# Packed attention and two mixtures on one core: first values in rows of nine tokens, a fold's copies in two turns, later keys by two queues

## The chip, the cores and the metric

The kernel runs on one core of a Trainium2 chip. The metric is the device time of one execution in microseconds (us). TensorE is called PE here (its weight loads PEld), VectorE DVE, ScalarE ACT, GpSimd POOL, SyncE SP.

## The reference

Four batches of eight heads attend to 576 tokens of 64 numbers through 32 packed queries p; the result, 2304 tokens by 512, goes through two layers of two matrices each. Cut to what matters:

```python
p_packed = sm_attn(p, k, v)                 # softmax(p k^T / 8) v: 32 rows a head
out = sm_attn(q, p_packed, p_packed)        # 576 rows a head
x = out.transpose(0, 2, 1, 3).reshape(2304, 512)
h = x @ moe_w_in;   g = h * tanh(log1p(exp(h)));   x = g @ moe_w_out     # d_ff 2048
h = x @ moe2_w_in;  g = where(h > 0, h, exp(h) - 1);  return g @ moe2_w_out
```

## The kernel before

Large matmuls are done in fp32r on a high and a low half of each operand: `split_hi` (L259) writes the high half, `split_lo` (L265, L267) the rest, and three products (high by high, high by low, low by high) stand for one.

**Attention of a batch.** `load_heads` (L348) brings k, q and v of two heads on 128 partitions. For batch 0, k and q come as rows (head, 64 groups of tokens) of nine tokens, 2304 contiguous bytes (L362); v comes by two DMAs a pair of heads (L355), five of the nine tokens to the first 64 partitions and four to the others (`RUNS`). `scores1` makes the scores of the packed queries and their exp (L463), one tile e1 for each half s of the heads; `transpose_a1` turns it on PE (L490) and copies it out, on DVE at L394 (ACT's copies are L392); `packed` multiplies by v (L515), scales, turns the result on PE and copies it to the tile PT, s by s. `scores2` multiplies the queries, transposed on DVE (L404), by PT (L569), turns the scores on DVE (`turn_s`, L598), and makes softmax and its split.

**First mixture.** The packed values are folded into the first matrix: `fold` (L651) multiplies PT by a quarter of w_in (matmul L662) and copies the two halves of the product out in two splits each (high: ACT, L259; low: DVE, L267). `gemm1` (L696 to L698), `mish` (t by ACT L706, gh by ACT L392, gl by DVE L714) and `gemm2` (L732 to L734) run in steps over 16 slices of d_ff and 8 blocks of 288 tokens. Meanwhile the second layer's first matrix is decoded into sums (w2c) and written to memory by POOL (`combine`, L321), and `reload_w1i` (L335) brings the first matrix again for the next batch's folds; y, the result of the first layer, is written by POOL too (L753).

**Second mixture.** `quartet` makes products over w2c (`product`, L828), elu, and splits; `gemm4` (L914) multiplies by the last matrix and, at the end, copies to ob (ACT L392, DVE L394 by turns) and writes out (L935). `second` decodes the last matrix in chunks of four raw tiles.

**What sets the order.** `startup` goes by the list `ORDER`, written by hand (r is a raw tile's load, L157; d a step of a decode, of which L194 is on ACT and L216 and L232 on DVE; 0T, 0V the turn and copy of e1, 0K the value products, 0P, 0U, 0W their scaling, turn and copy, 0S and 0t the second scores and their turn, f00 the first fold). Behind it `mixture1` and `mixture2` post closures in turn (a `Track` runs one post of a fold or of an attention step at a time), and a scheduler then places each instruction. A queue's instructions run in order; `pm` hands out the PSUM tiles.

## Time and profile before

| what | us |
|---|---|
| median of three runs | 779.54 |
| lowest and highest | 777.58, 779.99 |
| the profiled execution | 780.52 |
| its span in the trace | 778.7 |
| PE busy, DVE, ACT, POOL | 747.2, 529.1, 396.6, 104.3 |

The profile is of one execution. An engine is busy while an instruction of its own runs; a wait row names the instruction that waited and the one that released it; the chain of waits follows the last instruction back to its causes. The granted clock is a share of full speed: 1.00 is the 2.4 GHz level and 0.50 the 1.2 GHz level.

### The profile page before, as it was taken

To read this page: it belongs to the slowest core of one execution; us is meant where nothing else is said; L and a number is where in the kernel's file an instruction comes from. 1 tells how busy PE (TensorE), PEld (TensorE's weight loads), DVE (VectorE), ACT (ScalarE), POOL (GpSimd) and SP (SyncE) were. 2 spreads that over 40 slices of the span, in tenths; PEclk is the share of its full clock that TensorE was granted. 3 is DMA by queue.
4 is the path that set the end of the run, shared out by engine and by line. 5 is a ranking of instruction groups with operands and counts; after the bars stand their busy time and mean duration, and the time that the engine had idled before them with its cause. 6 is when DMAs were issued, how large, how long until landed. Compare 5 with 4: busy or idle time off the path is not lost.

```text
span 778.7 us, 13963 instructions
## 1 busy us (share of the span) xinstructions
PE 747.2 (96%) x5173; PEld 668.4 (86%) x5173; DVE 529.1 (68%) x1135; ACT 396.6 (51%) x840; POOL 104.3 (13%) x199
## 2 busy tenths in 40 slices
PE   7299999999999999999999999999999999999997
PEld 4198888898888988999998899888998889899985
DVE  5899977744953669886667878876455676545553
ACT  2799916473656457765644445534232354323332
POOL 1100000120120124752000003133000001000000
PEclk9699999999999999999999999999999999999999
DMA  8998746695483465877656325456343347333312
GB/s 283 412 358 262 186 101 193 181 253 159 112 253 77 126 202 182 281 234 247 233 199 202 116 109 196 155 189 204 109 115 122 102 139 240 108 110 116 128 54 82
DMA packets 95107, 138.81 MB, mean 178 GB/s; under 512 B 57920, under 2 KB 63616, under 8 KB 95040
## 3 DMA queue, kind: packets, MB, share of 16 engines
q1 hardware_dynamic: 83104, 105.73, 44.0%
q0 software_dynamic: 10208, 29.90, 10.5%
q10 hardware_dynamic: 1728, 2.29, 0.9%
q8 instruction: 41, 0.67, 0.4%
q14 instruction: 26, 0.21, 0.1%
HBM read 109.58 MB, written 28.31 MB: 177 GB/s over the span
## 4 chain that ended last, share of the span: by engine, by line
PE 79%; ACT 6%; DVE 6%; DMA 5%; issue 2%; SPq 1%; ACTq 0%; POOL 0%; DVEq 0%
PE o L914 24%; PE h L828 21%; PE acc L733 7%; PE acc L732 7%; PE acc L734 6%; PE h L696 3%; PE h L698 3%; PE h L697 3%; PE pm L662 2%; DMA w_dr<-w2c 2%; SPq L379 1%; DMA raw_w1i<-in_moe_w_in_dram 1%; ACT t L706 1%; ACT gh L259 1%; DMA k<-in_k_dram 1%
## 5 line engine op out<-in xcount | busy, mean ns | idle before, releaser
L828 PE MATMUL h<-y,w2c 128*128 128x384 f32 x1008 | 196.0, 337 | 1.8 <-ACT hs L392 1.2
L828 PEld LDWEIGHTS h<-y,w2c 128*128 128x128 f32 x1008 | 178.9, 188 | 12.3 <-ACT hs L392 2.0
L733 PE MATMUL acc<-gl,w1oh 128*128 128x288 f32 x512 | 151.1, 296 | 0.4 <-DVE gl L714 0.3
L734 PE MATMUL acc<-gh,w1ol 128*128 128x288 f32 x512 | 150.1, 295 | 0.0
L732 PE MATMUL acc<-gh,w1oh 128*128 128x288 f32 x512 | 148.7, 297 | 0.0
L914 PE MATMUL o<-w2ol,gh 128*128 128x512 f32 x288 | 113.0, 392 | 0.0
L914 PE MATMUL o<-w2oh,gh 128*128 128x512 f32 x288 | 109.1, 394 | 0.1
L914 PE MATMUL o<-w2oh,gl 128*128 128x512 f32 x288 | 108.1, 392 | 0.5 <-DVE gl L265 0.4
L733 PEld LDWEIGHTS acc<-gl,w1oh 128*128 128x128 f32 x512 | 96.1, 188 | 5.1 <-issue 2.3
L732 PEld LDWEIGHTS acc<-gh,w1oh 128*128 128x128 f32 x512 | 95.0, 188 | 6.0 <-issue 4.5
L734 PEld LDWEIGHTS acc<-gh,w1ol 128*128 128x128 f32 x512 | 96.0, 188 | 0.8 <-issue 0.8
L714 DVE TENSOR_TENSOR gl<-t,gh 128x288 fp32r<-128x288 f32 x128 | 57.2, 451 | 42.7 <-ACT gh L392 41.7
L696 PE MATMUL h<-a2h,gh 128*128 128x288 f32 x256 | 77.8, 304 | 3.5 <-ACT t L706 2.1
L706 ACT ACTIVATE t<-h 128x288 f32<-128x288 f32 x128 | 51.1, 405 | 56.0 <-PE h L698 53.2
L321 POOL DMA_DIRECT2D w_dr<-w2c x112 | 59.8, 540 | 138.0 <-DVE w2c L267 129.7
L698 PE MATMUL h<-a2h,gl 128*128 128x288 f32 x256 | 76.6, 300 | 0.0
L697 PE MATMUL h<-a2l,gh 128*128 128x288 f32 x256 | 76.4, 299 | 0.0
L259 ACT ACTIVATE gh<-t 128x384 fp32r<-128x384 f32 x96 | 49.6, 522 | 44.3 <-DVE t L839 42.5
L265 DVE TENSOR_TENSOR gl<-t,gh 128x384 fp32r<-128x384 f32 x96 | 52.8, 554 | 15.5 <-ACT gh L259 14.2
L914 PEld LDWEIGHTS o<-w2oh,gl 128*128 128x128 f32 x288 | 53.9, 188 | 10.9 <-DVE gl L265 1.2
L914 PEld LDWEIGHTS o<-w2ol,gh 128*128 128x128 f32 x288 | 54.1, 188 | 10.3
L392 ACT ACTIVATE gh<-t 128x288 fp32r<-128x288 f32 x112 | 49.4, 443 | 24.7 <-PE acc L734 22.8
(134 smaller groups left out, 1072.6 us busy)
## 6 DMA issues: line engine op xcount, KB each, us to landing
w2c<-w_dr SPq DMA_DIRECT2D x84, 512.0 KB, 3.6
w_dr<-w2c POOLq DMA_DIRECT2D x112, 128.0 KB, 3.3
w1r<-w_dr SPq DMA_DIRECT2D x24, 512.0 KB, 5.9
raw_w1i<-in_moe_w_in_dram SPq DMA_DIRECT2D x16, 512.0 KB, 10.5
raw_w1o<-in_moe_w_out_dram SPq DMA_DIRECT2D x16, 512.0 KB, 9.7
raw_w2i<-in_moe_w_in_dram SPq DMA_DIRECT2D x16, 512.0 KB, 4.3
raw_w2o<-in_moe_w_out_dram SPq DMA_DIRECT2D x16, 512.0 KB, 3.7
y_dr<-y POOLq DMA_DIRECT2D x16, 288.0 KB, 3.8
```

The lines of the kernel that those rows point to most:

```text
L259: nc.scalar.activation(out=hi, in_=val, func=ACTF.Copy, scale=factor)
L321: nc.gpsimd.dma_start(out=w2_dr[n // 2][:, n % 2, p], in_=d[x][:, i].bitcast(F32))
L696: nc.tensor.matmul(out=hp, lhsT=wh, rhs=xh, start=(kt == 0), stop=False)
L697: nc.tensor.matmul(out=hp, lhsT=wh, rhs=xl, start=False, stop=False)
L698: nc.tensor.matmul(out=hp, lhsT=wl, rhs=xh, start=False, stop=(kt == 1))
L706: nc.scalar.activation(out=d["t"], in_=d["h"], func=ACTF.Mish)
L714: nc.vector.tensor_tensor(out=gl, in0=d["t"], in1=gh.bitcast(F32), op=ALU.subtract)
L732: nc.tensor.matmul(out=o, lhsT=wh[:, cs], rhs=gh, start=first, stop=False)
L733: nc.tensor.matmul(out=o, lhsT=wh[:, cs], rhs=gl, start=False, stop=False)
L734: nc.tensor.matmul(out=o, lhsT=wl[:, cs], rhs=gh, start=False, stop=last)
L828: nc.tensor.matmul(out=hp, lhsT=w[:, p, a, :], rhs=y[:, b, :], start=start and p == 0 and i == 0, stop=p == 1 and i == 2, skip_group_check ...
L914: nc.tensor.matmul(out=o, lhsT=x[:, ts], rhs=y, start=(n == 1 and i == 0), stop=(n == NK and i == 2))
```

## The change

- Batch 0's v is loaded as k is, one DMA for a pair of heads, in rows of nine tokens. The exp tiles of batch 0 hold five and four groups of tokens for both halves s. A new function `values0` turns them (nine transposes for ten), multiplies by v in nine pieces of 64 rows for each head half (72 matmuls for 80) and copies PT once for twice.
- `whole`: a fold's copies are posted in two turns, high and low of one half, then of the other, in place of one.
- k of batches 2 and 3: of the DMAs of 32 x 9 x 32 (L379), those of the second 32 columns (x = 1) go by POOL.
- `product` and `gemm4` use one order for all blocks j: high by high, high by low, low by high. Before, block 2 of `gemm4` began with the low half of g.
- The last of the six final copies is done half by ACT, half by DVE.
- `second` asks for the raw tiles of the next chunk earlier.

```diff
 ORDER = """
-0k0 lq00 0k1 lq01 lq02 0k2 0k3 lq03 tp0 0A0 r0 0A1 0M0 r1 0E0 0M1 r2 0E1 0T0 0R0 0V0@ 0T1 0R1 r3 0K0 r4 0V1 r5
+0k0 lq00 0k1 lq01 lq02 0k2 0k3 lq03 tp0 0A0 r0 0A1 0M0 r1 0E0 0M1 r2 0E1 0T0 0R0 0T1 0V0@ 0R1 r3 r4 0V1 0K0 r5
...
-    def pm():
-        turn[0] += 1
-        if starting[0] and turn[0] % 3:
+    def pm(kind=None):
+        turn[0] += not kind
+        if kind == "a" or not kind and starting[0] and turn[0] % 3:
             t = ps_a.tile([128, 2, 512], F32, tag="acc", name="pm")
...
-        if nm == "v":
+        if nm == "v" and b:
             t = home([128, 2, 5, D], F32, f"{nm}{b}_{g}")
...
-                        eng.dma_start(
+                        (nc.gpsimd if x else eng).dma_start(
...
-            e1 = E1[b, s] = small([128, 5 * 128], F32, f"e1_{b}_{s}")
+            if not s or b:
+                E1[b, s] = small([128, 5 * 128], F32, f"e1_{b}_{s}")
+            if not s and not b:
+                E1[b, 1] = small([128, 5 * 128], F32, f"e1_{b}_1")
+            e1 = E1[b, s]
...
+                if not b:
+                    e1, r = E1[b, x], 64 * s
...
+    def values0():
+
+        d = {}
+        NC = NB // 2
+
+        def turn(x):
+            pm("a")
+            ps = d["t", x] = last_pair[0].rearrange("p h n -> p (h n)")
+            e1 = E1.pop((0, x))
+            for i in range(RUNS[x][2]):
+                cols = slice(128 * i, 128 * i + 128)
+                nc.tensor.transpose(out=ps[:, cols], in_=e1[:, cols], identity=ident)
+
+        def out(x, eng):
+            n = RUNS[x][2]
+            a1 = d["a", x] = small([128, n, 128], F32, f"a1t0_{x}")
+            evac(eng, a1, d["t", x][:, 0:n * 128].rearrange("p (c x) -> p c x", x=128))
+
+        def pe():
+            ps = d["k"] = pm("p")
+            for i in range(NC):
+                a1 = d["a", i // 5][:, i % 5, :]
+                for g in (3, 2, 1, 0):
+                    for s in range(2):
+                        r = slice(64 * s, 64 * s + 64)
+                        nc.tensor.matmul(
+                            out=ps[s][32 * g:32 * g + 32, 0:D], lhsT=a1[r, 32 * g:32 * g + 32],
+                            rhs=vt_in[0, g][r, 2 * i:2 * i + 2, :], start=(i == 0), stop=(i == NC - 1),
+                        )
+            for g in range(4):
+                vt_in.pop((0, g))
+
+        def scaled(s, eng="v"):
+            m = d["m", s] = st.tile([128, D], F32, tag="pv", name="pv")
+            rs = RS.pop((0, s))[:, 1:2]
+            if eng == "v":
+                nc.vector.tensor_scalar(out=m, in0=d["k"][s][:, 0:D], scalar1=rs, scalar2=None, op0=ALU.mult)
+            else:
+                nc.scalar.activation(out=m, in_=d["k"][s][:, 0:D], func=ACTF.Copy, scale=rs)
+
+        def turn2(s):
+            y = d["k"][0]
+            turns = [(slice(0, 64), 64 * s, 256)]
+            turns += [(slice(32 * x, 32 * x + 32), 64 * s + 32 * (1 - x), 384) for x in range(2)]
+            for cols, r, c in turns:
+                w = cols.stop - cols.start
+                nc.tensor.matmul(out=y[r:r + w, c:c + 128], lhsT=d["m", s][:, cols], rhs=ident)
+
+        def final(eng="v"):
+            PT[0] = ptp.tile([128, 256], F32, tag="pt", name="pt")
+            evac(eng, PT[0], d["k"][0][:, 256:512])
+
+        return turn, out, pe, scaled, turn2, final
...
-            d[0], d[1] = pm(), pm()
+            d[0], d[1] = pm("a"), pm("a")
...
-            for i, (a, b) in enumerate(((0, 0), (0, 1), (1, 0)) if j != 1 else ((0, 0), (1, 0), (0, 1))):
+            for i, (a, b) in enumerate(((0, 0), (0, 1), (1, 0))):
...
-            trio = [(gh, wh), (gh, wl), (gl, wh)]
-            if j == 1:
-                trio = [(gh, wh), (gl, wh), (gh, wl)]
-            if j == 2:
-                trio = [(gl, wh), (gh, wh), (gh, wl)]
-            for i, (x, y) in enumerate(trio):
-                nc.tensor.matmul(out=o, lhsT=x[:, ts], rhs=y, start=(n == 1 and i == 0), stop=(n == NK and i == 2))
+            nc.tensor.matmul(out=o, lhsT=gh[:, ts], rhs=wh, start=(n == 1), stop=False)
+            nc.tensor.matmul(out=o, lhsT=gh[:, ts], rhs=wl, start=False, stop=False)
+            nc.tensor.matmul(out=o, lhsT=gl[:, ts], rhs=wh, start=False, stop=(n == NK))
...
-                evac("av"[t % 2], ob, o)
+                if j == 2 and half and t == 2:
+                    evac("a", ob[:, 0:256], o[:, 0:256])
+                    evac("v", ob[:, 256:512], o[:, 256:512])
+                else:
+                    evac("av"[t % 2], ob, o)
...
-        for kt in range(2):
-            load_vt(0, kt)
+        for g in range(4):
+            load_heads(v, vt_in, 0, g, "v", (nc.sync, nc.scalar)[g % 2])
...
-                groups = (
-                    ("AMER", scores1(b, s)), ("TV", transpose_a1(b, s, "v")), ("KPUW", packed(b, s)),
-                )
+                groups = [("AMER", scores1(b, s))]
+                if b:
+                    groups += [("TV", transpose_a1(b, s, "v")), ("KPUW", packed(b, s))]
                 for names, fs in groups:
                     for n, f in zip(names, fs):
                         step(f"{b}{n}{s}", f, "a" if n in "VPW" else None)
+            if not b:
+                turned, copied, pe, scaled, turned2, final = values0()
+                for s in range(2):
+                    step(f"0T{s}", lambda s=s: turned(s))
+                    step(f"0V{s}", lambda eng="v", s=s: copied(s, eng), "a")
+                    step(f"0P{s}", lambda eng="v", s=s: scaled(s, eng), "a")
+                    step(f"0U{s}", lambda s=s: turned2(s))
+                step("0K0", pe)
+                step("0W0", final, "a")
...
-        for r in rows[:2]:
+        for r in rows[:2 if c < 2 else 0]:
...
-            if x < 2:
-                todo.append(lambda r=rows[x + 2]: load_raw("w2o", r, 0))
+            n = rows[x + 2] if x < 2 else 4 * (c + 1) + 2 * (x - 2)
+            if x < 2 or 0 < c < 3:
+                todo.append(lambda n=n: load_raw("w2o", n, 0))
...
-            return [f[0], lambda: [f[i]() for i in (1, 3, 2, 4)]]
+            return [f[0]] + [lambda x=x: (f[1 + x](), f[3 + x]()) for x in range(2)]
...
```

SP at the start, before (v and raw tiles are the values and the weights as they come; pr is p; ACT issues the other half in the same way):

```order
L362 DMA k_0_171<-in_k_dram 128x576
L362 DMA k_2_175<-in_k_dram 128x576
L993 DMA pr_149<-in_p_dram 32x4x64 x2
L355 DMA v_0_184<-in_v_dram 64x2x320
L355 DMA v_1_187<-in_v_dram 64x2x320
L355 DMA v_2_190<-in_v_dram 64x2x320
L355 DMA v_3_193<-in_v_dram 64x2x320
L362 DMA q_1_202<-in_q_dram 128x576
L362 DMA q_3_210<-in_q_dram 128x576
L157 DMA raw_w1i_0_230<-in_moe_w_in_dram 128x1024
```

and now:

```order
L362 DMA k_0_171<-in_k_dram 128x576
L362 DMA k_2_175<-in_k_dram 128x576
L1053 DMA pr_149<-in_p_dram 32x4x64 x2
L362 DMA v_0_184<-in_v_dram 128x576
L362 DMA v_2_188<-in_v_dram 128x576
L362 DMA q_1_198<-in_q_dram 128x576
L362 DMA q_3_206<-in_q_dram 128x576
L157 DMA raw_w1i_0_226<-in_moe_w_in_dram 128x1024
```

The four value issues of SP are two, in the form of the keys, and queries and raw tiles follow two issues earlier.

POOL at batch 3's keys, where one set of w2c ends and the next begins, before (y_dr is the first layer's result):

```order
L321 DMA w_dr_117<-w2c 128x256
L753 DMA y_dr_105<-y_0_2569 128x576
L753 DMA y_dr_105<-y_1_2573 128x576
L321 DMA w_dr_111<-w2c 128x256
L321 DMA w_dr_114<-w2c 128x256
```

and now:

```order
L321 DMA w_dr_117<-w2c 128x256
L813 DMA y_dr_105<-y_0_2582 128x576
L813 DMA y_dr_105<-y_1_2586 128x576
L379 DMA k_0_3049<-in_k_dram 32x9x32 x4
L379 DMA k_1_3058<-in_k_dram 32x9x32 x4
L379 DMA k_2_3129<-in_k_dram 32x9x32 x4
L379 DMA k_3_3138<-in_k_dram 32x9x32 x4
L321 DMA w_dr_111<-w2c 128x256
L321 DMA w_dr_114<-w2c 128x256
```

The half of the keys stands between y and the first w2c of the next set.

ACT at the last fold of batch 3, before (gh_3 is the fold's high half, t and gh the mish step):

```order
L259 ACTIVATE w2c<-dec 128x2x128
L259 ACTIVATE gh_3_3000<-pm 128x512 x2
L706 ACTIVATE t_3158<-h_3151 128x288
L392 ACTIVATE y_0_3176<-acc_2605 128x288
L392 ACTIVATE gh_3160<-t_3158 128x288
L392 ACTIVATE y_1_3180<-acc_2606 128x288
L706 ACTIVATE t_3196<-h_3189 128x288
```

and now:

```order
L259 ACTIVATE w2c<-dec 128x2x128
L259 ACTIVATE gh_3_3067<-pm 128x512
L392 ACTIVATE y_0_3199<-acc_2613 128x288
L392 ACTIVATE y_1_3203<-acc_2614 128x288
L259 ACTIVATE gh_3_3067<-pm 128x512
L766 ACTIVATE t_3219<-h_3212 128x288
L259 ACTIVATE w2c<-sums 128x2x128
```

The halves of gh_3 have both copies of y between them; t follows them as before.

## Rows read from the trace of the kernel before

**Rows 1.** The page: busy by engine; a PE group: busy, mean ns | idle before, releaser.

```profile
PE 747.2 (96%) x5173; PEld 668.4 (86%) x5173; DVE 529.1 (68%) x1135; ACT 396.6 (51%) x840; POOL 104.3 (13%) x199
...
L914 PE MATMUL o<-w2oh,gl 128*128 128x512 f32 x288 | 108.1, 392 | 0.5 <-DVE gl L265 0.4
```

**Rows 2.** The chain of waits, 0 to 60 us: start, length, what.

```profile
11.41 8.90 DMA raw_w1i<-in_moe_w_in_dram
```

**Rows 3.** Windows: PE, PEld, DVE, ACT, POOL busy, granted clock, DMA share, GB/s.

```profile
5.00:11.00 6.00, 4.61 (x71) 2.71 (x69) 4.57 (x9) 0.73 (x3) 0.00 (x0) 1.00 0.91 243
36.70:42.00 5.30, 5.21 (x28) 3.15 (x28) 5.15 (x11) 5.27 (x11) 0.82 (x2) 0.50 1.02 411
```

**Rows 4.** Issues of first values and keys: ns min/median/max, first to last start.

```profile
L355 SPq DMA_DIRECT2D v<-in_v_dram x9: 595/603/713, 4.7 to 61.4; - x9
...
L362 SPq DMA_DIRECT2D k<-in_k_dram x6: 328/328/416, 0.7 to 36.9; - x6
```

**Rows 5.** Timeline of PE, 11 to 34 us: start, length, work, [idle before <-releaser].

```profile
11.39 2.40 PE L490 MATMUL pm<-ident,e 128*128 128x128 f32 x10 [1.53 <-ACT e L463]
13.72 2.16 PE L515 MATMUL pm<-v,a1t 128*32 128x64 f32 x80
...
17.73 1.89 PE L569 MATMUL pm<-qT,pt 32*32 32x288 f32 x46 [0.58 <-DVE pt L394]
20.39 0.72 PE L569 MATMUL pm<-qT,pt 32*32 32x288 f32 x18 [0.76 <-issue]
33.57 1.11 PE L662 MATMUL pm<-w1v,pt 64*32 64x512 f32 x8 [12.45 <-DVE w1v L232]
```

**Rows 6.** Timeline of DVE, 13 to 23 us.

```profile
14.63 2.74 DVE L404 STREAM_TRANSPOSE qT<-q 128x576 f32<-128x576 f32 x4
17.30 0.84 DVE L394 COPY pt<-pm 64x256 f32<-64x256 f32 x2
...
21.03 0.43 DVE L216 TENSOR_SCALAR w1v<-raw_w1i 128x512 int32<-128x512 int32 x1 [1.65 <-ACT raw_w1i L194]
...
22.21 1.21 DVE L598 STREAM_TRANSPOSE x<-pm 128x288 f32<-128x288 f32 x3
```

**Rows 7.** Timelines of PE and ACT at 224 to 228 us.

```profile
227.24 0.40 PE L696 MATMUL h<-a2h,gh 128*128 128x288 f32 x1 [1.54 <-ACT t L706]
...
226.29 0.60 ACT L259 ACTIVATE gh<-pm 128x512 fp32r<-128x512 f32 x1 [0.76 <-DVE gl L267]
226.78 0.41 ACT L706 ACTIVATE t<-h 128x288 f32<-128x288 f32 x1
```

**Rows 8.** Chain at 150 to 170, PE at 166, waits of 210 to 230.

```profile
157.32 6.20 DMA w_dr<-w2c
...
167.24 0.76 PE L490 MATMUL pm<-ident,e 128*128 128x128 f32 x5 [0.84 <-ACT e L463]
...
ACT w2c L259 <- DMA w_dr<-w2c: 7.7, 3, 5.0
```

**Rows 9.** Later keys: issues, the window that holds most of batch 2's, SP's timeline.

```profile
L379 SPq DMA_DIRECT2D k<-in_k_dram x64: 312/453/1966, 110.2 to 221.1; - x64
...
125.30:140.10 14.80, 14.80 (x130) 13.02 (x128) 9.88 (x19) 6.71 (x16) 1.08 (x2) 1.00 0.69 171
...
208.79 0.35 SPq L157 DMA_DIRECT2D raw_w2i<-in_moe_w_in_dram  x1
209.18 12.42 SPq L379 DMA_DIRECT2D k<-in_k_dram  x20
```

**Rows 10.** POOL's w2c writes: issues, and the first of the second set.

```profile
L321 POOL DMA_DIRECT2D w_dr<-w2c x112: 539/539/559, 149.1 to 354.3; - x112
...
197.68 1.07 POOL L321 DMA_DIRECT2D w_dr<-w2c  x2 [11.49 <-DVE w2c L267]
```

**Rows 11.** The end: timelines of PE and ACT.

```profile
769.51 0.50 PE L914 MATMUL o<-w2oh,gl 128*128 128x512 f32 x1 [0.43 <-DVE gl L265]
...
773.00 1.57 ACT L392 ACTIVATE ob<-o 128x512 f32<-128x512 f32 x3 [1.89 <-DVE ob L394]
```

More of the change, by code (lines that the diff above doesn't have):

```diff
@@ L42 @@
 ORDER = """
-0k0 lq00 0k1 lq01 lq02 0k2 0k3 lq03 tp0 0A0 r0 0A1 0M0 r1 0E0 0M1 r2 0E1 0T0 0R0 0V0@ 0T1 0R1 r3 0K0 r4 0V1 r5
-0q0 0K1 0P0@ r6 0q1 0U0 0P1@ 0q2 r7 0q3 0U1 0W0 r8 d0.0 0W1 0S0 d0.1 r9 d0.3 d0.4 d1.0 d1.1 d1.3 d1.4 0t0 r10
-d2.0 0t1 d2.2 r11 0X2 d3.0 0X1 0Y2 r12 0N2 d4.0 d4.2 r13 0X0 0Y1 d5.0 0B2 0Y0 d2.1 d2.4 0H2 0N0 r14 d6.0 0L2
-0B0 r15 0X3 0H0 d7.0 0L0 0Y3 r16 d3.1 d7.2 d4.1 d8.0 d3.3 d3.4 r17 d4.4 d7.1 f00 d9.0 d8.1 d4.5 d9.2 d8.3 d8.4
-fh001 fh000 lk12 d9.1 d9.4 d10.0 fl000 d10.2 lk10 fl001 d11.0 d10.1 d10.4 g0 d11.2 lk13 d6.1 d12.0 d5.1 g1
@@ L48 @@
-d11.1 d11.4 m0 lk11 d6.3 f01 d5.3 m1 pr1 0N1 g2 h0 h1 fh011 g3 l0 m2 fl011 fh010 G0 h2 l1 d5.4 fl010 d13.0 r18
-d5.5 g4 lw100 l2 r19 0B1 m3 G1 m4 0N3 d6.4 d12.2 d6.5 r20 g5 d13.2 h3@ d12.1 G2 h4 m5 l3 d7.4 l4 r21 d12.4
-d7.5 g6 d15.0 r22 d12.5 G3 r23 d13.1 m6 0B3 0H1 d13.4 h5@ 0L1 g7 0H3 d13.5 d14.0 G4 0L3 h6@ 1k3 d14.2 l5 g8 m7
-r24 l6 d15.2 d14.1 G5 h7 d15.1 m8 r25 d14.4 l7 d15.4 g9 d14.5 h8 d15.5 d16.0 G6 1k0 m9 l8 d19.0 tp1 g10 G7 1k1
-m10 r26 h9 1k2 d19.2 l9 g11 d16.2 h10@ y7.0 d20.0 1A0 l10 r27 y7.1 y7.2 m11 g12 y7.3 d18.0 1M0 G8 d19.1 d19.4
@@ L53 @@
-m12 1E0 d18.1 g13 d20.1 G9 h11@ d18.3 d18.4 d17.0 l11 1R0 1A1 d16.1 d16.4 d17.2 d20.3 h12 G10 d17.1 d17.4 lv11
+0k0 lq00 0k1 lq01 lq02 0k2 0k3 lq03 tp0 0A0 r0 0A1 0M0 r1 0E0 0M1 r2 0E1 0T0 0R0 0T1 0V0@ 0R1 r3 r4 0V1 0K0 r5
+0q0 0P0@ r6 0q1 0U0 0P1@ 0q2 r7 0q3 0U1 0W0 r8 d0.0 0S0 d0.1 r9 d0.3 d0.4 d1.0 d1.1 d1.3 d1.4 0t0 r10 d2.0 0t1
+d2.2 r11 0X2 d3.0 0X1 0Y2 r12 0N2 d4.0 d4.2 r13 0X0 0Y1 d5.0 0B2 0Y0 d2.1 d2.4 0H2 0N0 r14 d6.0 0L2 0B0 r15
+0X3 0H0 d7.0 0L0 0Y3 r16 d3.1 d7.2 d4.1 d8.0 d3.3 d3.4 r17 d4.4 d7.1 f00 d9.0 d8.1 d4.5 d9.2 d8.3 d8.4 fh001
@@ new lines @@
+fh000 lk12 d9.1 d9.4 d10.0 fl000 d10.2 lk10 fl001 d11.0 d10.1 d10.4 g0 d11.2 lk13 d6.1 d12.0 d5.1 g1 d11.1
+d11.4 m0 lk11 d6.3 f01 d5.3 m1 pr1 0N1 g2 h0 h1 fh011 g3 l0 m2 fl011 fh010 G0 h2 l1 d5.4 fl010 d13.0 r18 d5.5
+g4 lw100 l2 r19 0B1 m3 G1 m4 0N3 d6.4 d12.2 d6.5 r20 g5 d13.2 h3@ d12.1 G2 h4 m5 l3 d7.4 l4 r21 d12.4 d7.5 g6
+d15.0 r22 d12.5 G3 r23 d13.1 m6 0B3 0H1 d13.4 h5@ 0L1 g7 0H3 d13.5 d14.0 G4 0L3 h6@ 1k3 d14.2 l5 g8 m7 r24 l6
+d15.2 d14.1 G5 h7 d15.1 m8 r25 d14.4 l7 d15.4 g9 d14.5 h8 d15.5 d16.0 G6 1k0 m9 l8 d19.0 tp1 g10 G7 1k1 m10
@@ L54 @@
+r26 h9 1k2 d19.2 l9 g11 d16.2 h10@ y7.0 d20.0 1A0 l10 r27 y7.1 y7.2 m11 g12 y7.3 d18.0 1M0 G8 d19.1 d19.4 m12
+1E0 d18.1 g13 d20.1 G9 h11@ d18.3 d18.4 d17.0 l11 1R0 1A1 d16.1 d16.4 d17.2 d20.3 h12 G10 d17.1 d17.4 lv11
 d25.0 l12 d26.0 1M1 d20.4 lv12 g14 d23.0 d25.1 d20.5 G11 1E1 lv10 d26.1 d25.3 d25.4 d24.0 lv13 1R1 f02 m13
```

## The prediction

> **What bounds the kernel now.** I read the page first: PE is busy 747.2 of 778.7 us [rows 1], so outside the start, the end and a few holes the time is PE's own work, and nearly all of that the change leaves alone (8 of the first batch's 80 value matmuls and one transpose go). Copies, DMAs and waits off PE therefore earn only where PE stands still; each part is judged by the PE hole that it touches. Four places have one.
>
> *The start, 0 to 36.7 us.* The chain of waits shows transfers first: the longest piece is a raw weight tile that is 8.90 us in flight [rows 2]. In the windows [rows 3] only 243 GB/s move from 5 to 11 us, when the values come in, and 411 later. The value DMAs take 0.60 us each to issue, the keys 0.33 [rows 4]. On PE [rows 5] transposes run from 11.39, value products from 13.72, the second scores from 17.73 to 21.11; then PE is idle 12.45 us until the first fold at 33.57. On DVE [rows 6] the query transposes (14.63, 2.74 us) end at 17.37, the copy of PT follows, a decode that begins at 21.03 has waited 1.65 us for a raw tile, and the turn of the scores starts at 22.21, behind that decode. From there DVE has hardly a gap up to the fold.
>
> *The clock.* From 36.7 to 42 us the granted clock is 0.50, the 1.2 GHz level, behind the long idle [rows 3]; later, as in 125.3 to 140.1, it is 1.00 [rows 9].
>
> *The middle.* PE stands 1.54 us at 227.24, because ACT did the two halves of a fold's copy one behind the other, 0.76 us of that waiting for DVE, with the mish step's t behind them [rows 7]. And 0.84 us at 167.24, where ACT had been held by a transfer of w2c [rows 8].
>
> *The end.* PE waits 0.43 us for gl at 769.51 [rows 11]; all PE idle ahead of that group is 0.5 us [rows 1]. Behind the last products come copies, three on ACT from 773.00 [rows 11].
>
> **The change, part by part.** The sum is made against the profiled execution, 780.52 us, 0.98 above the median of the three runs, 779.54.
>
> 1. *First values in rows of nine tokens.* Eight issues of 0.60 us become four of 0.33 [rows 4]; by two queues that is 4 x 0.60 - 2 x 0.33 = 1.7 us each. So queries and raw tiles are asked for up to 1.7 us earlier, into a stretch with spare bandwidth (243 of 411 GB/s), and the 1.65 us of DVE waiting for raw tile 1 can go. On PE one of ten transposes goes (2.40 / 10 = 0.24 us). The value products: 80 took 2.16 us, 20 turns of four column groups, 0.108 each [rows 5]; 72 are 18 such turns, 1.94 us, or, with the two row halves side by side, 9 turns, 0.97. Gain 0.2 to 1.2; I take the low end, since the row shows only column groups together. In the DVE rows the PT copy starts behind the query transposes, not behind PE, so PE's gain is covered by DVE. What DVE saves is one of two PT copies, 0.84 / 2 = 0.42 us [rows 6]. So the scores end at 21.11 - 0.42 = 20.69, and DVE would be ready at 22.21 - 1.65 - 0.42 = 20.14. The turn starts at the later, 20.7: **-1.5 us**, and the fold with it, as DVE is contiguous behind it. Bounds: -0.3 (raw tiles come no earlier; only small copies go) and -2.1 (also the scores earlier, the 20.14). The Trainium skill, TensorEngine Tiling (Array Packing), Tiling Modes, counts 64x32 as eight independent tiles; by that the products would take the 0.97, and if DVE is ready too, the start is at its -2.1 and the sum below at -3.55 in place of -2.95. No row shows two row halves side by side in the value products.
>
> 2. *The clock.* PE's 5.21 busy us at 0.50 [rows 3] would be 2.6 at full clock, so the low stretch costs 2.6. The idle ahead of it shrinks by 1.5 - 0.42 = 1.1 of 12.45 us; if the low stretch shrinks in that proportion, it gives back 0.09 x 2.6: **-0.2**. Bounds 0 (its length does not hang on the idle) and -1.3 (half of it goes).
>
> 3. *A fold's copies in two posts.* The same two copies, with other work between them. The order of ACT shows it: at the last fold of batch 3 both y copies now lie between the halves, where the 0.76 us wait was; elsewhere t. The 1.54 us hole is the only large one with this cause. But the rest of the order shifts too, and each displaced t can make a new hole: I charge 1.0 for these (the size of the 0.84 in rows 8). Net **-0.5**, bounds -2.5 (this hole and the 0.84 both go) and +3 (three or four new ones).
>
> 4. *Later keys by two queues.* 64 issues of 0.45 us on SP [rows 9]; 32 move to POOL, where an issue is 0.54 [rows 10]. In 125.3 to 140.1, with 26 of them, the DMAs are busy 0.69 at 171 GB/s and PE is busy for all of 14.80 us [rows 9]: no hole to win. **0**; its danger is rival D.
>
> 5. *One order of the output products.* gl last for the third block too. It is then needed two matmuls later than now, at 0.39 us of PE each [rows 1]; the 0.43 goes, and I take the group's whole **-0.5** [rows 1, 11], which is also the most (the least is 0).
>
> 6. *Last copy in two halves.* Three 512-wide ACT copies take 1.57 us, 0.52 each [rows 11]; half of one on each engine saves at most 0.26, less when a second instruction follows. **-0.25**, bounds 0 and -0.26.
>
> 7. *Earlier requests for the second output weights.* No PE hole in the trace is put down to them: **0**.
>
> Sum: -1.5 - 0.2 - 0.5 - 0.5 - 0.25 = -2.95; 780.52 - 2.95 = 777.57 for the profiled execution, less 0.98 is **776.6** against the median.
>
> **The rivals.**
>
> *B, the holes all go.* Start -2.1, clock -1.3, middle -2.4 (1.54 + 0.84), end -0.75: -6.55; 780.52 - 6.55 - 0.98 = 773.0. For it: DVE idles 1.65 us exactly at a raw tile, and the two holes have ACT as the releaser. Against: a scheduler that moves everything seldom takes away holes only.
>
> *C, the start's gain does not reach the fold.* The change does what it says, but raw tiles land as before, since at 411 GB/s each takes 1.28 us (128 x 1024 x 4 bytes) and a DMA waits for an older one; DVE then stands before another decode. Left are parts 3, 5 and 6, -1.25: 780.52 - 1.25 - 0.98 = 778.3. For it: from 36.7 the DMAs are full [rows 3], and a raw tile was 8.90 us in flight [rows 2]. Against: the 243 GB/s.
>
> *D, slower: POOL's keys hold back w2c.* In the order of POOL, batch 3's 16 key issues now stand between a batch's y writes and the first w2c writes of the next set. On SP that load stopped in its second tile, and 20 of its 32 issues went out from 209.18 on [rows 9]. If the third tile finds no buffer before that, POOL stops too: 8 issues x 0.54 = 4.3 us from 209.18 end at 213.5, and the first w2c write, now at 197.68 [rows 10], lies 15.8 us late. ACT waits for such writes already, three times 7.7 us in 210 to 230, 5.0 the longest [rows 8]; in front of its next w2c it stands with the mish steps behind it. A 6.20 us transfer ended in a PE hole of 0.84 [rows 8], so about 5.4 us are covered; past that each us is PE's: 15.8 - 5.4 = 10.4; 780.52 - 2.95 + 10.4 - 0.98 = 787.0. It gives a slower kernel from a hold of 5.4 + 2.95 = 8.35 us on, a third tile free later than 197.7 + 8.35 - 4.3 = 201.7. Against: on SP a raw tile stood ahead of those keys, issued at 208.79 [rows 9], and may be what they waited for; no raw tile goes by POOL. The Trainium skill, DMA: Bandwidth & Descriptors, SWDGE vs HWDGE vs iDMA, speaks against this part of the change in another way: descriptors of GpSimd's DMAs are written to rings in SBUF, from which VectorE in its two-port mode locks GpSimd out, while those issued by SP are immune. By that the issues on POOL would lengthen beside a busy DVE. The 112 issues there show none of it, 539 to 559 ns with DVE busy 68% [rows 1, 10], so it adds nothing to D.
>
> **How the numbers follow.** Forecast 0.55, B 0.16, C 0.18, D 0.11. About 0.3% (2.3 us) is what a measurement of this kernel can tell from no change, so faster means under 777.2. The forecast lies 0.6 below that and is given 0.82 of its chance there: 0.45 + B 0.16 = 0.61 faster. Same: the forecast's other 0.10, C 0.18, and 0.01 of D (a small hold): 0.29. Slower: D's other 0.10. The range goes from B less 0.5, 772.5, to C with 2 us of new holes in place of 1 and half the spread of the three runs (2.41 / 2), 778.3 + 1.0 + 1.2 = 780.5; it leaves out D and the tail of B.
>
> **What would show it.** Right: the turn of the scores at about 20.7 us, the first fold near 32.1; PE idle there some 11 us; no hole of 1.5 us by a t near 225; no wait for gl at the end; last PE end to end of span 0.2 us shorter. C: the fold at 33 or later with a DVE wait for a raw tile. D: POOL's third key tile issued after 202 us, ACT waiting over 5 us for w_dr behind it, and PE idle. The prediction is wrong if the fold is later than 33.6, or if the PE holes between 60 and 700 us add up to over 2 us more than before.

## The result, and the profile after

The changed kernel takes 790.03 us (median of five, 788.13 to 790.28), the kernel before 779.54 in the same comparison (median of five, 777.58 to 784.60): ratio 1.0126, 95% interval 1.0086 to 1.0166, 1.3% slower. The forecast was 776.6, the range 772.5 to 780.5. The profiled executions have spans of 788.5 and 778.7 us, and the following goes by these.

The page after, busy time by engine and the group of gl products (columns as in [rows 1]):

```profile
PE 749.3 (95%) x5237; PEld 670.5 (85%) x5237; DVE 528.4 (67%) x1134; ACT 395.7 (50%) x839; POOL 124.1 (16%) x231
...
L970 PE MATMUL o<-w2oh,gl 128*128 128x512 f32 x288 | 101.3, 393 | 0.0
```

PE's busy time is 2.1 us up, the span 9.8: the time went into holes. And PE has 64 matmuls more than in [rows 1], where the prediction took 8 and one transpose away. POOL has 32 more, the keys.

The start, PE's timeline after (columns as in [rows 5]):

```profile
14.06 1.87 PE L513 MATMUL pm<-v,a1t 64*32 64x64 f32 x140
19.90 0.43 PE L513 MATMUL pm<-v,a1t 64*32 64x64 f32 x4 [3.96 <-issue]
20.73 1.26 PE L534 MATMUL pm<-ident,pv 128*64 128x128 f32 x6 [0.40 <-ACT pv L526]
22.40 1.26 PE L534 MATMUL pm<-ident,pv 128*64 128x128 f32 x6 [0.41 <-ACT pv L526]
24.25 2.59 PE L629 MATMUL pm<-qT,pt 32*32 32x288 f32 x64 [0.59 <-DVE pt L394]
38.28 1.96 PE L722 MATMUL pm<-w1v,pt 64*32 64x512 f32 x16 [11.43 <-DVE w1v L232]
```

The trace has 144 records for the 72 value matmuls that the program calls, two each. So it was before: `packed` calls 40 for batch 0 (five chunks by four groups, for two halves), and its 80 in [rows 5] are their records. (The second scores are 32 calls and 64 records too; a transpose is one record, 10 calls and 10 records.) So "72 matmuls for 80" sets calls against records: the change raises the calls from 40 to 72. PE stops for 3.96 us four records before the end of the values, and "issue" means that it waits for nothing the profile shows. The second scores start at 24.25 instead of 17.73, the fold at 38.28 instead of 33.57: 4.7 us.

DVE's timeline after, the same stretch:

```profile
14.77 2.75 DVE L404 STREAM_TRANSPOSE qT<-q 128x576 f32<-128x576 f32 x4
23.78 0.42 DVE L394 COPY pt<-pm 128x256 f32<-128x256 f32 x1 [6.26 <-PE pm L534]
24.12 0.42 DVE L216 TENSOR_SCALAR w1v<-raw_w1i 128x512 int32<-128x512 int32 x1
...
26.93 1.57 DVE L658 STREAM_TRANSPOSE x<-pm 128x288 f32<-128x288 f32 x4 [0.60 <-PE pm L629]
```

What was forecast of DVE is there (one PT copy of 0.42 for two; no wait for a raw tile, the first of which landed at 15.43 instead of 17.52), but DVE waits 6.26 us for PE.

Windows after (columns as in [rows 3]):

```profile
5.00:11.00 6.00, 4.70 (x71) 2.72 (x69) 4.47 (x9) 0.70 (x3) 0.00 (x0) 1.00 1.04 340
20.70:24.00 3.30, 2.52 (x12) 0.96 (x12) 0.22 (x1) 1.96 (x5) 0.00 (x0) 0.50 1.04 418
36.70:42.00 5.30, 2.47 (x18) 0.76 (x18) 4.70 (x9) 4.65 (x10) 1.28 (x2) 0.50 1.08 378
520.00:523.60 3.60, 1.77 (x10) 1.27 (x8) 2.06 (x5) 0.57 (x2) 0.00 (x0) 0.99 0.75 262
523.60:527.00 3.40, 3.40 (x11) 3.11 (x11) 3.33 (x9) 2.26 (x5) 0.00 (x0) 0.51 0.48 160
```

From 5 to 11 us 340 GB/s move instead of 243. Behind the stop the twelve turns run at a granted clock of 0.50, the 1.2 GHz level: 0.21 us each.

The middle, PE's timeline after:

```profile
170.10 0.72 PE L426 MATMUL pm<-kT,pD 64*32 64x288 f32 x16 [2.32 <-ACT e L469]
...
192.79 0.40 PE L792 MATMUL acc<-gh,w1oh 128*128 128x288 f32 x1 [0.77 <-DVE y L394]
...
522.40 3.33 PE L888 MATMUL h<-y,w2c 128*128 128x384 f32 x12 [1.83 <-DVE r L938]
```

The holes at 170.10 and 192.79 are new (0.84 at 167.24 before [rows 8]); the 1.54 at 227.24 [rows 7] is gone. Ahead of the third stand these rows of POOL's and DVE's timelines (yr is a part of y, read back):

```profile
516.67 0.56 DVE L265 TENSOR_TENSOR gl<-t,gh 128x384 fp32r<-128x384 f32 x1
521.32 0.56 DVE L841 TENSOR_TENSOR yr<-yr 128x384 f32<-128x384 f32 x1 [4.09 <-DMA yr<-y_dr]
...
515.88 3.23 POOL L828 DMA_DIRECT2D yr<-y_dr  x6 [17.14 <-DVE gl L265]
```

POOL's load of yr goes out at 515.88, though DVE had read the old contents of that buffer by 513.00, 2.88 us earlier; before, the same load went out 0.29 us behind DVE's read.

The same matmuls, set side by side in the two traces, show where the 9.8 us arose:

| stretch | after against before, us |
|---|---|
| up to the first products (36.8) | +4.7, then level to 144 us |
| 144 to 330 us | +0.7 (some +3.5 at 186 to 222, given back by 245) |
| near 380 us | +0.8 |
| 494 to 527 us | +3.7 |
| 527 to the last product | -0.8 |
| behind the last product | +0.55 |

### The profile page after: what moved, and what is told of

It reads as the page before. It is cut to its first block, busy times and chain, and to the rows that moved or that the text cites. A ratio compares the mean times of both kernels' runs of the same rounds, so it can differ in the third digit from the quotient of the medians.

```text
span 788.5 us, 14116 instructions
## 1 busy us (share of the span) xinstructions
PE 749.3 (95%) x5237; PEld 670.5 (85%) x5237; DVE 528.4 (67%) x1134; ACT 395.7 (50%) x839; POOL 124.1 (16%) x231
## 4 chain that ended last, share of the span: by engine, by line
PE 76%; DVE 7%; ACT 6%; DMA 6%; issue 3%; POOL 1%; SPq 0%; ACTq 0%; DVEq 0%; POOLq 0%
PE h L888 22%; PE o L968 8%; PE o L970 8%; PE o L969 8%; PE acc L792 6%; PE acc L793 6%; PE acc L794 6%; PE h L756 3%; PE h L757 3%; PE h L758 2%; DMA yr<-y_dr 2%; PE pm L722 2%; DMA w_dr<-w1v 1%; DMA raw_w2i<-in_moe_w_in_dram 1%; ACT t L766 1%
## 5 line engine op out<-in xcount | busy, mean ns | idle before, releaser
L888 PE MATMUL h<-y,w2c 128*128 128x384 f32 x1008 | 199.2, 339 | 3.5 <-DVE r L938 1.8
L968 PE MATMUL o<-w2oh,gh 128*128 128x512 f32 x288 | 114.0, 396 | 0.1
L970 PE MATMUL o<-w2oh,gl 128*128 128x512 f32 x288 | 101.3, 393 | 0.0
L968 PEld LDWEIGHTS o<-w2oh,gh 128*128 128x128 f32 x288 | 54.3, 188 | 9.8 <-ACT gh L259 0.5
```

What stands on the lines that cost most here:

```text
L888: nc.tensor.matmul(out=hp, lhsT=w[:, p, a, :], rhs=y[:, b, :], start=start and p == 0 and i == 0, stop=p == 1 and i == 2, skip_group_check ...
L968: nc.tensor.matmul(out=o, lhsT=gh[:, ts], rhs=wh, start=(n == 1), stop=False)
L970: nc.tensor.matmul(out=o, lhsT=gl[:, ts], rhs=wh, start=False, stop=(n == NK))
```

## The experiments

Each run is compared with the kernel before on its own chip; the ratio stands with its 95% interval.

### The start

**First values as before** (all of part 1 undone).

```diff
+    for kt in range(2):
+        load_vt(0, kt)
-        for g in range(4):
-            load_heads(v, vt_in, 0, g, "v", (nc.sync, nc.scalar)[g % 2])
...
```

> The changed kernel with the first batch's values as before, all else as changed. Theory (the values part alone costs the start): the first fold is back at 33.6 us from 38.3, PE's stop with no releaser is 0.8 us in the second scores instead of 4.0 us in the value products, and the time falls by about 4.7 us, to about 785. Rival (the other parts disturb the start, or the lost start is regained later): the fold stays near 38, or it moves and the time falls by less than 2 us.

Measured: 784.33 us, ratio 1.0053 (1.0025 to 1.0081); the three other versions on that chip, all with the new values, 1.0110 to 1.0135. First fold at 32.42, PE's stop 0.51 us, inside the second scores. So part 1 costs some 5 us; the rest of the change is slower than before too.

**Scaling ahead of the first turn** (in `ORDER`, so that both turns run together).

```diff
-0q0 0P0@ r6 0q1 0U0 0P1@ 0q2 r7 0q3 0U1 0W0
+0q0 0P0@ r6 0q1 0P1@ 0U0 0q2 r7 0q3 0U1 0W0
```

> The changed kernel with one step moved: the scaling of the second half (0P1 on ACT) ahead of the turn of the first half (0U0 on PE), in the hand-written order. Theory (the second scaling waited 1.36 us for the first turn, since both are in one tile): the two turns run together, PT is copied 1.3 to 1.7 us earlier, the first fold comes at about 36.8 instead of 38.3, and the time falls by 1.3 to 1.6 us. Rival (what holds the start is DVE or the raw tiles behind it): the fold moves by less than 0.3 us.

Measured: 788.29, 1.0110 (1.0075 to 1.0145); the stop is 4.26 us, the fold at 38.24, so the theory fails. The two waits of 0.4 us by the turns are one of 0.61, but nothing comes of it.

**What the stop is.** PE's records ahead of it, from windows that end there, before and after (PE's and PEld's counts are those in brackets):

```profile
0.00:19.63 19.63, 13.82 (x220) 8.84 (x221) 11.02 (x23) 5.36 (x14) 2.76 (x9) 0.91 0.89 284
```

```profile
0.00:15.94 15.94, 10.26 (x222) 7.49 (x223) 7.46 (x16) 4.03 (x10) 2.76 (x9) 0.89 0.90 308
```

441 and 445; with 8 and 4 records of semaphores, which the view leaves out, it is the 449th in both. The 0.76 us "issue" in [rows 5] was this stop. In both traces one transfer of 16,384 bytes on the instruction queue ends 1.3 us before PE goes on (before 18.11 to 19.07, after 17.62 to 18.62). The DMA view of 17.6 to 18.65 us after has it:

```profile
q8 instruction: 1, 0.02, 6.0%
```

So two theories stood: PE reaches the end of what it holds of its program 3.7 us earlier (N: the next part is asked for too late for it), or the transfer is slowed by the raw tiles that now come earlier (Q).

**Raw tiles held** behind the first exponentials (a tiny DMA that needs their sums goes first on SP).

```diff
-0k0 ... 0A0 r0 0A1 0M0 r1 0E0 0M1 r2 0E1 0T0 0R0 0T1 0V0@ 0R1 r3 r4 0V1 0K0 r5
+0k0 ... 0A0 0A1 0M0 0E0 0M1 0E1 0T0 0R0 0T1 0V0@ 0R1 hold r0 r1 r2 r3 0V1 r4 0K0 r5
+            nc.sync.dma_start(out=y_dr[7][0:1, 0, 0:2], in_=RS[0, 1][0:1, 0:2])
```

> The changed kernel with one tiny DMA on SP (two numbers into a scratch tensor that is written over later) that waits for the sums of the first scores at about 12.8 us; the raw weight tiles, which were asked for from 8.3 us on, are asked for behind it. Theory Q (the instruction transfer that ends the stop at 17.6 to 18.6 us was asked for long before, and waits behind the raw tiles): it comes by 15 us, PE's stop of 4.0 us shrinks to below 2. Theory N (it is asked for only when PE is nearly out of instructions, and takes some 2 us): it comes at 17 to 19 us as before and the stop stays between 3 and 5 us. The time by either is not lower by the same amount, since the raw tiles land 3 to 4 us later and DVE decodes two of them ahead of the turn of the scores.

Measured: 788.5, 1.0063 (1.0035 to 1.0091). The raw tiles land from 17.02 on (15.43), the transfer runs from 17.39 to 18.33, and PE's timeline keeps the stop:

```profile
19.64 0.43 PE L513 MATMUL pm<-v,a1t 64*32 64x64 f32 x4 [4.02 <-issue]
```

Q falls.

**Small matmuls added ahead of the first exponentials' turn**, whose result nothing reads: 64 in the kernel before, then 64 in the changed one.

```diff
+            for i in range(64):
+                g = i % 4
+                nc.tensor.matmul(
+                    out=wu[32 * g:32 * g + 32, 0:64], lhsT=ident[:, 32 * g:32 * g + 32], rhs=ident[:, 0:64],
+                )
```

> The kernel before with 64 small matmuls added (each one weight load and one matmul, 128 PE instructions, output unused) behind the first scores, where PE is idle from 9.5 to 11.4 us. Theory (PE runs out of fetched instructions after 449 of them, and goes on 1.3 us after the transfer of the next 16 KB of instructions has ended): the stop without a releaser comes 128 instructions earlier, in the value products near 15.7 us, lasts until about 20 us (some 4 us instead of 0.8), the first fold comes some 4 us later, and the time is 3 to 5 us above the kernel before. Rival (the stop belongs to the new 64-row products, not to the number of instructions): no stop over 1.5 us, fold within 1 us of 33.6, time within 1 us of before.

Measured: 783.53, 1.0031 (0.9989 to 1.0074). They are 128 matmuls and 128 loads in the trace, 256 records, not the 128 expected. PE's timeline has two stops, at its 449th and 705th record:

```profile
16.80 1.61 PE L515 MATMUL pm<-v,a1t 128*32 128x64 f32 x71 [2.65 <-issue]
...
22.99 0.72 PE L569 MATMUL pm<-qT,pt 32*32 32x288 f32 x18 [1.27 <-issue]
```

The fold starts at 35.18, 1.6 later, and the time is not clear of noise. But in the kernel before too, the stop goes where the count puts it.

> The changed kernel with 64 small matmuls (128 PE instructions, output unused) added behind the first scores, where PE is idle. Theory (PE asks for its next 16 KB of instructions some 5.3 us before it can go on, at about the 265th, and the new products burn the rest in 2 us): the request falls before the transposes, the stop at the 449th shrinks from 4.0 to about 1.7 us, the second scores end near 23.5 us instead of 26.8, the first fold comes near 35 instead of 38.3, and the time falls by 2.5 to 4.5 us although work was added. Rival (the stop is the price of the 64-row products themselves): the stop stays over 3.5 us, the fold is not earlier, the time is the same or higher.

Measured, the changed kernel: 792.31, 1.0136 (1.0104 to 1.0167). With 256 records and not 128 added, this was one whole period: the second stop falls where the first one was, and the fold is at 40.16. PE's timeline:

```profile
15.87 1.69 PE L513 MATMUL pm<-v,a1t 64*32 64x64 f32 x128 [2.14 <-issue]
21.79 0.42 PE L513 MATMUL pm<-v,a1t 64*32 64x64 f32 x4 [4.24 <-issue]
```

**Half as many** (`range(32)`, 128 records), behind the first scores.

> The changed kernel with 32 small matmuls (each has four PE records, 128 in all; output unused) behind the first scores. Theory (PE asks for 256 instructions at a time, some 5.3 us before it can go on, and stops at the 449th and the 705th where it uses them up faster): the first stop falls into the value products at about 15 us with 1.5 us, the second into the second scores and is short; these end near 24 us instead of 26.8, the first fold comes near 35.5 instead of 38.3, and the time falls by 2 to 3.5 us. Rival (any pad moves all of it later): fold not earlier than 38, time the same or higher.

Measured: 785.69, 1.0073 (1.0047 to 1.0099), on a chip where the changed kernel with another edit has 1.0133. PE's timeline:

```profile
15.39 0.88 PE L513 MATMUL pm<-v,a1t 64*32 64x64 f32 x68 [1.15 <-issue]
16.68 0.78 PE L534 MATMUL pm<-ident,pv 128*64 128x128 f32 x6 [0.41 <-ACT pv L526]
...
33.75 1.96 PE L722 MATMUL pm<-w1v,pt 64*32 64x512 f32 x16 [11.45 <-DVE w1v L232]
```

and its clock in a window:

```profile
17.00:24.00 7.00, 3.42 (x75) 1.35 (x74) 4.09 (x10) 3.19 (x6) 0.68 (x1) 1.00 1.03 415
```

Useless work makes the kernel 4.5 us faster at the fold. The stops are 1.15 and 0.88 us, because the transfers now begin at 13.08 and 19.10, and the clock stays at 1.00, so that the turns take 0.13 us each. That the transfer is PE's own next part of the program is argued from this, not shown: no record names its engine. And even so the fold is no earlier than the 33.57 before.

### The hole at 520 us

**Output weights asked for as before** (part 7 undone).

```diff
-        for r in rows[:2 if c < 2 else 0]:
+        for r in rows[:2]:
...
```

> The changed kernel with the second output matrix's raw tiles asked for as before. Theory (the earlier raw tiles hold the buffers that the loads of y need): the PE hole of 2.0 us near 520 us and the 3.4 us at half clock behind it go, and the time falls by 3 to 4 us, to about 786.5. Rival (the order of the output products holds the buffers): the hole stays and the time moves by less than 1 us.

Measured: 790.23, 1.0135 (1.0104 to 1.0167). The hole stays, 1.64 us ahead of 523.6, as the rival forecast. Its cause, the order of the output products, is not shown by that: the added DMAs below take the hole away with that order kept.

**Later keys by SP alone** (part 4 undone).

```diff
-                        (nc.gpsimd if x else eng).dma_start(
+                        eng.dma_start(
```

> The changed kernel with all later keys on SP again. Theory (the keys on POOL put the w2c writes and with them ACT later near 160 to 178 us): the holes of PE of 2.3 us near 170 and 1.1 us near 177 shrink to below 1.2 us together and the time falls by 1 to 2.5 us. Rival (those holes come from the order that the split fold gives): they stay within 0.5 us and the time stays within 1 us of the changed kernel's 790.0.

Measured: 789.04, 1.0131 (1.0079 to 1.0183). No hole near 520, but one of 4.71 us ahead of 238.5. The two holes near 170 and 177 are 2.32 us together instead of 3.40, between theory and rival. So the place of the keys matters, though the sum stays.

**Is it a count on POOL?** 24 tiny memsets on POOL at the start; then, in another run, 18 small DMAs on POOL, which went out at 110 to 176 us (32 columns of the second PT, to memory that is not read).

```diff
+            for _ in range(24):
+                nc.gpsimd.memset(z[:, 0:1], 0)
```

> The changed kernel with 24 tiny memsets added on POOL at the very start, where it is idle (zeros onto zeros); nothing else. Theory (POOL too waits for instructions near 513 us: a transfer of 8 KB of them starts at 513.2, and POOL goes on 2.2 us after its end; 32 more key DMAs shifted the place where that falls to the loads of y that PE needs): the place moves 24 instructions earlier, into an idle stretch, the loads of y go out at 513 and 515.5 instead of both from 515.9, the 2.0 us hole near 520 and the half clock behind it go, and the time falls by 3 to 4 us. Rival (the buffers of y come free later in this order of work): the hole stays at 1.8 to 2.2 us and the time stays within 1 us of the changed kernel.

Measured: 789.87, 1.0104 (1.0073 to 1.0135); the hole stays, 1.79. Other instructions do not move it. That is what the rival forecast, but not for its cause, the buffers of y, as the next run shows.

```diff
+            for i in range(18):
+                nc.gpsimd.dma_start(out=y_dr[7][:, 0, 0:32], in_=PT[1][:, 0:32])
```

> The changed kernel with 18 more DMAs on POOL near 100 to 150 us (128 rows of 128 bytes each into a part of y's scratch tensor that is written over later). In all kernels with keys on POOL its 78th and its 184th DMA went out 2.1 and 2.9 us after what they wait for; without keys on POOL only its 113th did. Theory (POOL stops for 2 to 3 us at places that the DMAs issued before it fix): the 184th is now one of the last w2c writes near 355 us, nobody waits for it, the hole near 520 us goes and the time falls by 3 to 4 us, less what the 18 DMAs disturb. Rival (the loads of y wait for something else that the keys delay): the hole stays at 1.8 to 2.2 us.

Measured: 789.71, 1.0133 (1.0107 to 1.0159). The hole is gone; POOL's timeline has the loads in two groups again, as before:

```profile
516.51 1.62 POOL L828 DMA_DIRECT2D yr<-y_dr  x3 [14.55 <-DVE y L265]
518.65 1.62 POOL L828 DMA_DIRECT2D yr<-y_dr  x3 [0.52 <-DVE y L265]
```

In the changed kernel, and in each of the nine runs with half of the keys on POOL and no DMAs added, two of POOL's DMAs go out late, by 2.06 or 2.07 us and by 2.87 or 2.88 behind the last DVE work that they wait for: those with 78 and 184 others ahead of them (in the changed kernel at 276.01 us, where nothing waits, and at 515.88). With the 18 in between it is those with 78 and 176, at 226.18 and 362.27 us. In the kernel before, and wherever the keys are on SP, it is the one with 113, at 341.36 us before, where it does no harm. No instruction transfer of 4 KB or more falls in the 6 us ahead of that one, so this is not the kind of stop that PE had. So POOL pauses at places that its earlier DMAs set, and the 32 key DMAs moved a pause into the one load that PE soon needs. The 3.1 us won at 520 were lost again, mostly ahead of 145.76, to a hole of 2.10 where DVE waits 4.7 us for keys.

### The fold's copies, and the rest

**Copies in one turn** (part 3 undone).

```diff
-            return [f[0]] + [lambda x=x: (f[1 + x](), f[3 + x]()) for x in range(2)]
+            return [f[0], lambda: [f[i]() for i in (1, 3, 2, 4)]]
```

> The changed kernel with a fold's copies in one turn as before. Theory (the split fold made the new holes near 170 us): the 2.3 us hole near 170 goes, the 1.5 us hole by the mish step near 230 comes back, and the time changes by less than 1.5 us. Rival (the split fold is worth its 1.5 us and cost nothing): the time rises by 1 to 2 us.

Measured: 787.35, 1.0052 (1.0029 to 1.0074), beside 1.0063 for the held raw tiles on the same chip. In place of the holes ahead of 170.10 (2.32) and 192.79 (0.77) there is one of 1.27, ahead of 171.19. So the split costs 1 to 2 us (1.8 by 260 us with the same matmuls set side by side, 1.2 by the times, whose intervals overlap). A third hole of the changed kernel, 1.08 ahead of 177.37, is gone as well, but only four of the nine traces with the split and half of the keys on POOL have it. And there is no hole near 225 either, though the copies are in one turn.

**Parts 5, 6 and 7 alone**, in the kernel before.

> The kernel before with the change's last parts alone: the order of the output products, the last copy in two halves, the earlier raw tiles. Theory: they are worth the PE waits for gl, 0.2 to 0.6 us each at 615, 642, 766 and 769 us, less the 0.3 us that the last copy lost: -0.5 to -1.0 us, with the first fold and the hole near 225 us as before. Rival (the earlier raw tiles take what POOL's loads of y need): a hole near 515 us and 2 to 4 us above the kernel before.

Measured: 779.2, 0.9976 (0.9945 to 1.0008). No hole near 515, so the rival falls; the gain is not clear of noise. The hole near 225 is missing too, where the theory kept it.

### Put together

**Old values, one turn, the 24 memsets on POOL.** The forecast was 777 to 779 us and no hole over 1.5 us behind 60 us. Measured: 783.07, 1.0017 (0.9994 to 1.0040). The hole near 515 stays with 2.81 us, as the memsets do not move POOL's pause; nor is there any hole over 0.6 us elsewhere behind 60 us, so the rival (keys on POOL cost by themselves, with holes near 160 to 235) falls too.

**Old values, one turn, 18 POOL DMAs early** (the DMAs as above).

> The changed kernel with the first batch's values and the fold's copies as before, and the 18 more DMAs on POOL: keys on two queues, the order of the output products, the halved last copy and the earlier raw tiles stay. Theory: the first fold at 32.4 to 33.6 us, no hole near 225 us, none near 515, span 776 to 778, so 0.3 to 0.6% below the kernel before, whose hole near 225 varies. Rival (POOL's stops fall where ACT waits for w2c): a new hole of over 1.5 us between 150 and 360 us, time as before or above.

Measured: 783.67, 1.0049 (1.0023 to 1.0075). No hole at 225 nor at 515, but others ahead of 139.80 (1.43), 161.93 (3.11) and 191.94 (0.68), as the rival said.

**The same with the 18 DMAs late**, at 370 to 434 us, when POOL has little else to do.

```diff
+                if j == 0 and q == 1:
+                    for i in range(18):
+                        nc.gpsimd.dma_start(out=w1_dr[0][:, 0, 0:32], in_=yop[0, 0, 0][:, 0, 0:32].bitcast(F32))
```

> The changed kernel with the old first values and the fold's copies in one turn, and 18 small DMAs issued by POOL at about 380 to 400 us (128x32 of a split operand of the second mixture, to memory that nothing reads any more), when POOL has little else to do. Theory (POOL pauses at places set by the DMAs it issued before): no hole of 1.5 us or more at 505 to 525 us, and, as the DMAs now come behind the writes of w2c, none of the holes of 0.8 to 3.3 us at 138 to 191 us that 18 earlier ones brought; no hole near 225 us; first fold 32 to 34 us; profiled span 774.5 to 777.5; ratio to before 0.995 to 1.000. Rival (the hole near 515 us has another cause, and the 18 DMAs removed it by chance): the hole stays, 2 to 3 us; ratio 1.000 to 1.004.

Measured: 779.7, 0.9978 (0.9954 to 1.0002), span 778.8. POOL's timeline:

```profile
430.23 0.54 POOL L1239 DMA_DIRECT2D w_dr<-y  x1 [4.25 <-issue]
...
507.83 1.63 POOL L768 DMA_DIRECT2D yr<-y_dr  x3 [15.06 <-DVE y L265]
```

The pause falls on one of the added DMAs, again the one with 184 ahead of it, and the loads of yr go out on time: the theory, at the place it named. The span is 1.3 over its bound, and a hole of 1.71 ahead of 166.19, which the theory ruled out, is there.

**The changed kernel with all three repairs**: one turn, 32 small matmuls, late DMAs; and the same with the keys on SP and no added DMAs.

> The changed kernel with the fold's copies in one turn, 32 small matmuls (128 records) behind the first scores as in the run that had these alone, and the 18 late DMAs on POOL: new first values, both of their costs moved away. Theory (the start's loss is PE's stop after its 449th record and the half clock behind it, the loss at 520 us is POOL's pause, the rest is the split fold): first fold 33 to 35 us, no hole of 1.5 us at 505 to 525, profiled span 775 to 779, ratio 0.995 to 1.002. Rival (the new values cost PE or DVE time of their own further on): span over 780, ratio over 1.003.

Measured: 781.81, 0.9996 (0.9970 to 1.0022), span 779.8, fold at 35.54. Same as before, then, and not better; fold and span lie 0.5 and 0.8 past the bounds, with a stop of 1.87 us.

> The changed kernel with the fold's copies in one turn, all later keys by SP again, and the 32 small matmuls behind the first scores: the new values with their stop moved, without anything new on POOL. Theory: first fold 33 to 35 us, no hole of 1.5 us at 505 to 525, and before's hole at 220 to 235 us back (1.5 to 4 us); span 775 to 780, ratio 0.997 to 1.003. Rival (keys on POOL are not what removes the hole near 225): no hole of over 1 us at 215 to 235.

Measured: 783.06, 1.0022 (0.9991 to 1.0052), span 785.0 and fold at 35.59, 5.0 and 0.6 past the bounds. Before's hole is back; PE's and ACT's timelines:

```profile
231.67 0.61 PE L756 MATMUL h<-a2h,gh 128*128 128x288 f32 x1 [3.80 <-ACT t L766]
...
229.06 0.42 ACT L259 ACTIVATE w2c<-dec 128x256 fp32r<-128x256 f32 x1 [4.33 <-DMA w_dr<-w2c]
229.38 0.58 ACT L259 ACTIVATE gh<-pm 128x512 fp32r<-128x512 f32 x1
230.72 0.60 ACT L259 ACTIVATE gh<-pm 128x512 fp32r<-128x512 f32 x1 [0.76 <-DVE gl L267]
```

The 0.76 us between the copies is that of [rows 7], but ahead of it ACT stood 4.33 us for a write of w2c. The run with parts 5 to 7 alone has the same 0.76, and no hole of PE there. ACT's timeline in it:

```profile
223.11 0.60 ACT L259 ACTIVATE gh<-pm 128x512 fp32r<-128x512 f32 x1 [0.76 <-DVE gl L267]
```

What differs is how long ACT waits for writes of w2c in all. The waits of 205 to 240 us (sum, times, longest), in that run and in the one just above, which has the hole of 3.80:

```profile
ACT w2c L259 <- DMA w_dr<-w2c: 5.6, 4, 2.8
ACT w2c L259 <- DMA w_dr<-w2c: 9.7, 3, 4.4
```

With 7.7 [rows 8] the hole is 1.54, with the 9.5 of the 64 small matmuls in the kernel before 3.56; in the changed kernel there is no such wait, and no hole.

The hole near 225 us (from 205 to 245, of 0.6 us or more), as copies and keys go:

| | keys on SP | half of them on POOL |
|---|---|---|
| copies in one turn | 1.54 [rows 7], 3.56 and 3.80; none with parts 5 to 7 alone | none, five runs |
| copies in two turns | 4.71 | none, eight runs and the changed kernel |

Each cell goes by one execution of a kernel. The times of all executions say the same: the five kernels with all keys on SP spread by 6.8 to 11.2 us on a chip (before, 777.13 to 785.73 in one comparison), the fourteen with half of them on POOL by 1.8 to 3.7. And the trace without the hole is of that kernel's quickest execution (776.05 of 776.05 to 785.28), the one with 4.71 of the slowest (794.19 of 785.93 to 794.19). That the hole is what makes the spread fits this and is not shown.

## Why the prediction was wrong

Both signs that were named for a wrong prediction came: the fold is later than 33.6 us (38.28), and PE's holes between 60 and 700 us add up to 10.0 us where they were 5.9.

*Part 1 (forecast -1.5; measured +4.7 up to the fold).* The value DMAs, the raw tiles (2.1 us earlier) and the saved copy came as worked out. The step that failed is "80 took 2.16 us ... 72 are 18 such turns, 1.94 us": the 80 are records of the trace, for 40 calls, and the 72 are calls, which make 144 records. So part 1 adds 64 matmuls and 64 loads to PE, where the step took 8 matmuls away. PE comes to its 449th record 3.7 us sooner, before the next transfer has begun, and stands for 3.96 us, a term that the sum did not have. That 1.94 us came out as a duration (144 records take 1.88 in the run with 32 small matmuls) is luck. At nearly the same granted clock, 140 records took 1.87 us (0.77) and the 80 of before 2.16 (0.76), 13 ns each for 27: the two row halves do run side by side, which the prediction had as its cheaper reading, and twice the records use that up. The stop that should have warned stood in the rows I quoted, "0.76 <-issue" [rows 5], and I gave it no cause. A second thing was missed: the new turns wait twice for the scaling (0.40 and 0.41), so from the last value product to the second scores it is 3.0 us at full clock in that run, where [rows 5] have 1.9. In no run with the new values does the fold start before the 33.57 of [rows 5].

*Part 2 (-0.2).* The clock was lost where I did not look: 0.50 behind the stop, some 1.0 us in the turns (twelve at 0.21 us for 0.13).

*Part 3 (-0.5).* The hole of [rows 7] was put down to "one behind the other". The runs take that away: with the keys on POOL the hole is absent with either order of the copies, with the keys on SP it is there with either, in four traces of five, and the fifth has the 0.76 us between the copies without the hole. What grows with the hole is ACT's waiting for writes of w2c ahead of the copies. The charge of 1.0 for new holes was too small: those ahead of 170.10, 177.37 and 192.79 make 4.2 us where before had 0.84, some 1.8 of it due to the split.

*Part 4 (0; rival D feared it).* Both were wrong. The keys on POOL removed the hole at 225. Rival D's condition, a third key tile after 202 us, was met (twelve issues from 202.32), but the w2c steps themselves came later with it (first write of the second set at 220.99, for 197.68): ACT waits for no write of w2c in 210 to 235 us (7.7 us in [rows 8]). What cost time was POOL's pause 300 us later, 3.7 us with the half clock behind it, which nothing in the trace of before showed at that place.

*Part 5 (-0.5): right.* The group of gl products has 0.0 us of idle time ahead of it for 0.5 [rows 1].

*Part 6 (-0.25): half right.* The last copy ends 0.71 us behind the last matmul, where it was 0.93. But the last output DMA (the fourth on SP; in the kernel before, ACT's last) goes out 0.93 behind it instead of 0.96 and takes 3.18 us instead of 2.86. DVE's and SP's timelines after:

```profile
782.63 1.18 DVE L394 COPY ob<-o 128x256 f32<-128x256 f32 x2 [0.85 <-ACT ob L392]
...
780.78 3.64 SPq L995 DMA_DIRECT2D out_dram<-ob  x4
```

*Part 7 (0).* Undoing it changed nothing that could be seen.

In sum: +4.7 up to the fold, +3.7 from the pause, +1.8 from the split, +0.8 near 380 us and +0.55 at the end, less 1.5 at 225 and 0.8 behind 527, where the gl waits were, make 9.3 of the 9.8. The cause of the 0.8 near 380 us was not tried.

No version beats the kernel before for certain: the best two, parts 5 to 7 alone (0.9976) and the change without new values and split, with the late DMAs (0.9978), both have intervals that reach 1. The 0.3% that the prediction held for enough to tell from no change is too fine for single executions: those of the kernel before lie between 777.1 and 786.2 us.
